# First loads of a retention kernel as two half-height transfers, issued from two engines

## The chip, the cores and the metric

The kernel runs on one core of a Trainium2 chip. The metric is device time in microseconds (us) of one execution, as a median of runs; lower is better. A core has TensorE (PE in the rows; its weight loads are PEld), VectorE (DVE), ScalarE (ACT), GpSimd (POOL), SyncE (SP, which here only issues transfers), and sixteen DMA engines that move data between device memory and the core.

## What is computed

The reference is a gated linear recurrence over 768 tokens (2 batches, 8 heads of 64), followed by two MLPs of 512 to 2048 to 512 on the resulting 1536 tokens:

```python
for t in range(S):
    state = gamma * state + einsum('bhd,bhe->bhde', k[:, :, t], v[:, :, t])
    y[:, :, t] = scale * einsum('bhd,bhde->bhe', q[:, :, t], state)
x = y.transpose(0, 2, 1, 3).reshape(1536, 512)
h = x @ w_in;  x = (h * tanh(softplus(h))) @ w_out
h = x @ w2_in; out = (h * cos(h)) @ w2_out
```

## The kernel before

The recurrence is done in twelve chunks of 128 tokens, six for each batch. A chunk's data are one row of the array `qkv`, 128 partitions by 2048 columns of float32 (1 MB): columns 0 to 1023 hold q and k transposed ("qk"), 1024 to 1535 hold v, 1536 to 2047 hold k in natural order ("k"). Here qk0 means qk of chunk 0, and so on; a qk load is 512 KB, a v or a k load of chunks 0 and 1 is 256 KB. From chunk 2 on v and k come as one load of 512 KB (vk2, vk3, ...). The constants ("few", 146 KB) come first; VectorE grows the causal mask from them, and GpSimd the decay factors.

For each chunk TensorE makes

- scores (`att_scores`, tile ps_s): needs qk; VectorE then multiplies the mask in (tile p);
- out (`att_out`, tile ps_y from p): needs p and v;
- update (`att_update`, tile ps_u): the running state, needs k and vd, which is v times a decay, made by GpSimd or, for chunks 1, 2, 4, 7 and 9, by ScalarE in eight instructions, one for each head;
- inter (`att_inter`, tile ps_y from qd and st): needs qd, made by GpSimd from q, and the state st of the chunk before.

After the twelve chunks (about 44 us) TensorE multiplies for the MLPs (tiles ps_h and ps_o) to the end. The MLP weights come through the same queue as the chunks; two weight loads stand among the chunk loads.

Every step is entered with `op(engine, cost, function, ...)` into a planner (`Plan`), which works out from the costs in what order the program is written; each engine then runs its instructions in that order. Loads are entered with engine "SP" and keep the order in which they are entered. All transfers of the kernel before are issued by SyncE and go through one hardware queue. Eight completion semaphores (DMAHW0 to DMAHW7 in the order below) are taken in turn, so a transfer can be issued only when the one eight places ahead of it has landed.

At the start there is nothing for TensorE to do: `start_up` gives it 24 multiplications of zeros (line 794), and the line `op("PE", 0.9, zeros, 8, "u")` puts 8 more between scores of chunk 0 and scores of chunk 1.

Of the kernel before, what the change touches and what calls it, by code (L numbers as in the profile page):

```python
# [10 lines left out]
F32 = mybir.dt.float32  # L11
F32R = mybir.dt.float32r
# [12 lines left out]
BLK = 512  # L25
# [46 lines left out]
class Plan:  # L72
# [15 lines left out]
    def op(self, engine, cost, fn, *args, needs=(), uses=(), new=None):  # L88
        n = len(self.ops)
        uses = list(uses)  # L90
        before = set(needs)
        reuse = None
        if new is not None:
            key, bufs, *tag = new
            line = self.lines.setdefault(tag[0] if tag else key[0], [])
            if line:
                before.add(self.owner[line[-1]])
            if len(line) >= bufs:
                reuse = line[-bufs]
            line.append(key)  # L100
            self.owner[key] = n
            uses.append(key)
        for key in uses:
            if self.owner.get(key, n) != n:
                before.add(self.owner[key])
            self.users.setdefault(key, set()).add(n)
        if engine in self.given:
            before |= {self.last[engine]} if engine in self.last else set()
            self.last[engine] = n
        att = fn.__name__.startswith("att") or fn.__name__ in ("start_up", "zeros", "load_consts")  # L110
        self.ops.append(dict(engine=engine, cost=cost, fn=fn, args=args, before=before, reuse=reuse, att=att))
        return n
# [64 lines left out]
def retention_two_mlps(ctx: ExitStack, tc: tile.TileContext, qkv, w1i, w1o, w2i, w2o, consts, out):  # L177
    nc = tc.nc
# [6 lines left out]
    g_p = ctx.enter_context(tc.tile_pool(name="g", bufs=3))  # L185
# [81 lines left out]
    att = {}  # L267
# [10 lines left out]
            x_t[m, j] = x_p.tile([128, 2, KD, BLK], F32R, tag="x", name="x")  # L278
        return x_t[m, j]

    def att_load(g, lo, hi, eng=nc.sync):
        if not att:
            t = x_p.tile([128, 2, KD, BLK], F32R, tag="x", name="qkv")
            for n in range(2):
                att[n] = t[:, n].rearrange("p a b -> p (a b)").bitcast(F32)
        elif g in IN_WO and g not in att:
            t = wo_p.tile([128, 2, 2, 512], F32R, tag="wo", name="qkv")
            att[g] = t.rearrange("p a b c -> p (a b c)").bitcast(F32)
        elif g in IN_G and g not in att:
            t = g_p.tile([128, 2, 2, BLK], F32R, tag="g", name="qkv")  # L290
            att[g] = t.rearrange("p a b c -> p (a b c)").bitcast(F32)
        elif g not in att:
            att[g] = att_p.tile([128, 2048], F32, tag="qkv", name="qkv", bufs=3)
        eng.dma_start(out=att[g][:, lo:hi], in_=qkv[g, :, lo:hi])  # L294

    def qk_of(g):
        return att[g][:, 0:1024].rearrange("p (a q b) -> p a q b", a=NPAIR, q=2)
# [237 lines left out]
    op = plan.op  # L535
# [48 lines left out]
    def chunk(g):  # L584
        return ("qkv", max(g, 1))

    def chunk_loads(g, cuts, queue=nc.sync):
        key = chunk(g)
        for lo, hi in zip(cuts, cuts[1:]):
            n = op(  # L590
                "SP", (hi - lo) * (0.00142 if g < 3 else 0.00122), att_load, g, lo, hi, queue,
                uses=[key], new=None if key in plan.owner else (key, 3, "x" if g < 2 else "wo" if g in IN_WO else "g" if g in IN_G else "qkv"),
            )
            for part, last in (("qk", 1024), ("v", 1536), ("k", 2048)):
                if lo < last and hi > last - 512:
                    at.setdefault((part, g), []).append(n)

    def chunk_pre(g):
        c = g % NCH
        key = chunk(g)  # L600
        on_act = g in VD_ACT
        if c + 1 < NCH:
            at["vd", g] = [
                op(
                    *(("ACT", 0.98) if on_act else ("POOL", 1.15)), att_vd, g, part, needs=at["v", g] + at["dec"],
                    new=None if part else (("vd", g), 2), uses=[key, ("vd", g)],
                )
                for part in range(2 if on_act else 1)
            ]
        if c > 0:  # L610
            name, cost, eng = ("DVE", 0.72, nc.vector) if g in QD_DVE else ("POOL", 1.95, nc.gpsimd)
            at["qd", g] = op(
                name, cost, att_qd, g, eng, needs=at["qk", g] + at["decq"], new=(("qd", g), 2), uses=[key]
            )
# [4 lines left out]
    def chunk_scores(g):  # L619
        s = [("s", g, e) for e in range(2)]  # L620
        if g == 1:
            s = [("s", g)] * 2
            at["s", g] = op("PE", 1.05, att_scores, g, needs=at["qk", g], new=(s[0], 1, "y"), uses=[chunk(g)])
        else:
            first = op(None, 0.0, nothing, new=(s[0], 3, "s"))
            at["s", g] = op("PE", 1.05, att_scores, g, needs=at["qk", g] + [first], new=(s[1], 3, "s"), uses=[chunk(g), s[0]])
        for e in range(2):
            at["p", g, e] = at["p", g] = op(
                "DVE", 0.71, att_mask, g, e, needs=[at["s", g]] + at["mask"],
                new=None if e else (("p", g), 2), uses=[s[e], ("p", g)],  # L630
            )
# [119 lines left out]
    few_t = []  # L751
# [7 lines left out]
        late_h_p = ctx.enter_context(tc.tile_pool(name="late_h", bufs=1, space=PSUM))  # L759
        o_p = ctx.enter_context(tc.tile_pool(name="o", bufs=2, space=PSUM))  # L760

    def load_consts():
        t = g_p.tile([128, 2, 2, BLK], F32R, tag="g", name="few").rearrange("p a b c -> p (a b c)").bitcast(F32)
        few_t.append(t)
        nc.sync.dma_start(out=t[:, 0:292], in_=consts[:, 0:292])  # L765

    def few(lo, n):
        return few_t[0][:, lo : lo + n]
# [22 lines left out]
    def zeros(n, tag):  # L791
        ps = ps_p.tile([128, 256], F32, tag=tag, name="ps_w")
        for _ in range(n):
            nc.tensor.matmul(ps, zero, zero[:, 0:1].to_broadcast([128, 256]), start=True, stop=True)

    def start_up():
        nc.vector.memset(zero, 0.0)
        nc.vector.memset(quarter, 0.25)
        nc.vector.memset(magic, MAGIC)
        nc.scalar.activation(out=spare, in_=quarter, func=AF.Copy, scale=quarter)  # L800
        zeros(2 * WARM, "u")

    at["close"] = op(None, 0.0, close)
    op("PE", 5.5, start_up)
    load = op("SP", 0.4, load_consts, new=("few", 3, "g"))
    chunk_loads(0, (0, 1024))
    for g in range(2):
        chunk_loads(g, (1024, 1536))
        chunk_loads(g + 1 + g, (0, 1024))
        chunk_loads(g, (1536, 2048))  # L810
        if g == 0:
            chunk_loads(2, (0, 1024))

    def later_loads(gs):
        for g in gs:
# [30 lines left out]
    for n in range(2):  # L846
        chunk_pre(n)
        chunk_scores(n)
        if n == 0:
            op("PE", 0.9, zeros, 8, "u")  # L850
    for n in range(NCHK):
        if 0 < n < NCHK - 1:
            chunk_pre(n + 1)
# [116 lines left out]
```

## Time and profile before

| | us |
|---|---|
| median of 3 runs | 571.52 (571.49 to 572.43) |
| the profiled execution's own time | 571.26 |
| span of the profiled execution, first to last instruction | 569.5 |
| TensorE busy in the span | 565.0 (99%) |
| VectorE, ScalarE, GpSimd busy | 384.4, 226.8, 97.7 |
| DMA queue q1, share of 16 engines' span | 23.6% |

The 1.8 us between the span and the profiled execution's time lie before the first and behind the last instruction of the program. The shares are averages over stages that differ much: in the first 42 us the DMA engines work without a break for most of the time, later they are mostly idle.

### The profile page before, as it was taken

The page shows a single profiled execution, that of the slowest core. Times are in us where ns is not written, and L with a number is a line of the kernel's source. Part 1 is how long each engine was busy: PE and PEld are TensorE (multiplying, and loading weights), DVE is VectorE, ACT ScalarE, POOL GpSimd, SP SyncE. Part 2 cuts the span into 40 slices and gives each one's busy share as a digit, 9 for nine tenths or more (in the row PEclk, how much of TensorE's full clock was granted, in tenths as well). Part 3 has the DMA queues.
Part 4 walks back from the last instruction along what each step waited for, and adds up shares of the span by engine and source line. Part 5 has one row for each costly group of instructions (what it writes and reads, how often), then busy time and mean ns, then how long its engine had stood idle before and what let it go on. Part 6 is the DMA issues. An engine that isn't in the chain of part 4 may idle for free.

```text
span 569.5 us, 7240 instructions
## 1 busy us (share of the span) xinstructions
PE 565.0 (99%) x3052; PEld 469.0 (82%) x3052; DVE 384.4 (67%) x420; ACT 226.8 (40%) x268; POOL 97.7 (17%) x74
## 2 busy tenths in 40 slices
PE   8999999999999999999999999999999999999997
PEld 6888888888888888888888888888888888888886
DVE  6689899652465527563487976898498894765462
ACT  2565443331312302304326466366246354354240
POOL 6770001111110201111101111122010311010000
PEclk9999999999999999999999999999999999999999
DMA  8982154421042200312022120303004100000203
GB/s 295 403 352 83 70 218 148 148 103 46 1 147 75 74 1 7 142 74 75 0 75 75 48 100 1 147 1 147 1 0 148 39 36 1 0 1 0 75 37 112
DMA packets 15008, 49.90 MB, mean 88 GB/s; under 512 B 1664, under 2 KB 2048, under 8 KB 14976
## 3 DMA queue, kind: packets, MB, share of 16 engines
q1 hardware_dynamic: 14976, 49.44, 23.6%
q8 instruction: 24, 0.39, 0.3%
q14 instruction: 8, 0.07, 0.0%
HBM read 46.29 MB, written 3.15 MB: 87 GB/s over the span
## 4 chain that ended last, share of the span: by engine, by line
PE 98%; DMA 1%; SPq 0%; DVE 0%; issue 0%
PE ps_h L431 46%; PE ps_o L454 46%; PE ps_y L384 2%; PE ps_s L329 2%; DMA qkv<-qkv_dram 1%; PE ps_y L374 1%; PE ps_u L345 1%; SPq L294 0%; DVE acc L520 0%; SPq L765 0%
## 5 line engine op out<-in xcount | busy, mean ns | idle before, releaser
L431 PE MATMUL ps_h<-x,wi 128*128 128x512 f32 x1152 | 264.8, 389 | 0.0
L431 PEld LDWEIGHTS ps_h<-x,wi 128*128 128x128 f32 x1152 | 216.2, 188 | 45.0 <-issue 0.2
L454 PE MATMUL ps_o<-wo,g 128*128 128x512 f32 (+1 forms) x588 | 132.5, 385 | 0.0
L454 PE MATMUL ps_o<-g,wo 128*128 128x512 f32 x576 | 132.4, 389 | 0.0
L454 PEld LDWEIGHTS ps_o<-wo,g 128*128 128x128 f32 x588 | 108.9, 188 | 22.0
L454 PEld LDWEIGHTS ps_o<-g,wo 128*128 128x128 f32 x576 | 108.1, 188 | 22.4
L262 POOL TENSOR_TENSOR wo<-mag,wo 128x1024 fp32r<-128x1024 f32 x14 | 35.8, 2559 | 211.4 <-ACT wo L248 158.4
L497 DVE TENSOR_TENSOR g<-mish,g 128x1024 fp32r<-128x1024 f32 x24 | 33.4, 1393 | 55.0 <-ACT g L493 55.0
L513 DVE TENSOR_TENSOR acc<-ps_o,acc 128x1024 f32<-128x1024 f32 x35 | 42.8, 1222 | 34.6 <-PE ps_o L454 34.4
L262 POOL TENSOR_TENSOR wi<-mag,wi 128x1024 fp32r<-128x1024 f32 x12 | 30.3, 2526 | 193.1 <-ACT wi L248 193.1
L464 ACT ACTIVATE mish<-ps_h 128x1024 f32<-128x1024 f32 (+1 forms) x25 | 24.9, 995 | 95.7 <-PE ps_h L431 95.7
L477 DVE SCALAR_TENSOR_TENSOR turns<-whole,turns 128x1024 f32<-128x1024 f32 x24 | 29.3, 1223 | 44.7 <-ACT whole L473 44.7
L469 ACT ACTIVATE turns<-ps_h,quarter 128x1024 f32<-128x1024 f32 x24 | 26.7, 1113 | 65.4 <-PE ps_h L431 65.1
L239 DVE SCALAR_TENSOR_TENSOR mag<-raw,mag 128x1024 uint32<-128x1024 uint32 (+1 forms) x38 | 42.2, 1111 | 1.2
L486 ACT ACTIVATE turns<-turns 128x1024 f32<-128x1024 f32 x24 | 25.5, 1062 | 34.8 <-DVE turns L483 34.6
L497 DVE TENSOR_TENSOR g<-turns,g 128x1024 fp32r<-128x1024 f32 x24 | 33.2, 1383 | 8.0 <-ACT g L493 8.0
L489 DVE TENSOR_TENSOR turns<-turns,ps_h 128x1024 f32<-128x1024 f32 x24 | 29.2, 1216 | 10.1 <-ACT turns L486 6.8
L254 DVE SCALAR_TENSOR_TENSOR mag<-raw,mag 128x1024 uint32<-128x1024 uint32 x26 | 33.8, 1301 | 0.4
L493 ACT CAST g<-turns 128x1024 fp32r<-128x1024 f32 x24 | 25.1, 1045 | 17.0 <-DVE turns L489 16.8
L248 ACT CAST wi<-mag 128x1024 fp32r<-128x1024 f32 (+1 forms) x20 | 17.4, 872 | 26.5 <-DVE mag L254 22.4
L473 ACT ACTIVATE whole<-turns,magic 128x1024 f32<-128x1024 f32 x24 | 27.7, 1153 | 0.8
L483 DVE TENSOR_SCALAR turns<-turns 128x1024 f32<-128x1024 f32 x24 | 27.0, 1126 | 0.8
(50 smaller groups left out, 326.6 us busy)
## 6 DMA issues: line engine op xcount, KB each, us to landing
qkv<-qkv_dram SPq DMA_DIRECT2D x22, 512.0 KB, 10.0
raw<-w1i_dram SPq DMA_DIRECT2D x16, 512.0 KB, 4.2
raw<-w1o_dram SPq DMA_DIRECT2D x16, 512.0 KB, 4.1
raw<-w2i_dram SPq DMA_DIRECT2D x16, 512.0 KB, 3.7
raw<-w2o_dram SPq DMA_DIRECT2D x16, 512.0 KB, 3.7
out_dram<-acc SPq DMA_DIRECT2D x11, 256.0 KB, 2.1
qkv<-qkv_dram SPq DMA_DIRECT2D x4, 256.0 KB, 7.1
out_dram<-acc SPq DMA_DIRECT2D x2, 128.0 KB, 1.7
```

The lines of the kernel that those rows point to most:

```text
L239: nc.vector.scalar_tensor_tensor(out=a, in0=high, scalar=0xC0000000, in1=a, op0=ALU.bitwise_and, op1=ALU.bitwise_or)
L254: nc.vector.scalar_tensor_tensor(out=w_all_of(it, single)[:, ns], in0=raw_t[it][:, ns, :, 0], scalar=29, in1=mag_t[it][:, ns], op0=ALU.log ...
L262: eng.tensor_sub(out=w[:, :, 1], in0=w_all_of(it, single)[:, ns].bitcast(F32), in1=w[:, :, 0].bitcast(F32))
L431: nc.tensor.matmul(h[:, 0 if h_tag(k) == "s" else f % 2, :], w[:, f % 2, a, kk * 128 : (kk + 1) * 128], x[:, b, kk, :], start=(a + b + kk ...
L454: nc.tensor.matmul(ps, lhs, rhs, start=(n == 0), stop=(n == 3 * GF - 1))
L469: nc.scalar.activation(out=t_t[k], in_=h_t[k], func=AF.Identity, scale=INV_2PI, bias=quarter)
L473: nc.scalar.activation(out=n_t[k], in_=t_t[k], func=AF.Identity, bias=magic)
L477: nc.vector.scalar_tensor_tensor(out=t, in0=n_t[k], scalar=MAGIC, in1=t, op0=ALU.subtract, op1=ALU.subtract)
L483: nc.vector.tensor_scalar(out=t, in0=t, scalar1=-0.5, scalar2=0.5, op0=ALU.max, op1=ALU.min)
L489: nc.vector.tensor_mul(out=t_t[k], in0=t_t[k], in1=h_t[k])
L497: nc.vector.tensor_sub(out=g[:, :, 1, :], in0=t_t[k], in1=g[:, :, 0, :].bitcast(F32))
L513: nc.vector.tensor_add(out=acc, in0=o_t[m * NG + G, j, p], in1=acc)
```

## The change

The constants and qk0, qk1 and qk2 are each loaded by two transfers, partitions 0 to 63 by SyncE and partitions 64 to 127 by ScalarE. k0 stays one transfer and is issued by ScalarE. The order becomes few, qk0, qk1, then v0 (SyncE) and k0 (ScalarE), qk2, v1, qk3, k1; before it was few, qk0, v0, qk1, k0, qk2, v1, qk3, k1. ScalarE issues its five transfers at the head of `start_up`. The 8 multiplications of zeros ahead of scores of chunk 1 become 4. The planner's cost of an early load goes from 0.00142 to 0.0013 us a column.

```diff
+    early = []
+    issued = set()
+    EVERY, UPPER, LOWER = slice(0, 128), slice(0, 64), slice(64, 128)
+
-    def att_load(g, lo, hi, eng=nc.sync):
+    def att_load(g, lo, hi, eng=nc.sync, at_rows=EVERY):
...
-        eng.dma_start(out=att[g][:, lo:hi], in_=qkv[g, :, lo:hi])
+        if (g, lo, hi, at_rows) not in issued:
+            eng.dma_start(out=att[g][at_rows, lo:hi], in_=qkv[g, at_rows, lo:hi])
+            issued.add((g, lo, hi, at_rows))
...
-    def chunk_loads(g, cuts, queue=nc.sync):
+    def chunk_loads(g, cuts, queue=nc.sync, at_rows=EVERY):
...
-                "SP", (hi - lo) * (0.00142 if g < 3 else 0.00122), att_load, g, lo, hi, queue,
+                "SP", (hi - lo) * (0.0013 if g < 3 else 0.00122) * share, att_load, g, lo, hi, queue, at_rows,
...
+            if queue is not nc.sync:
+                early.append((g, lo, hi, queue, at_rows))
...
-    def load_consts():
+    def load_consts(eng=nc.sync, at_rows=UPPER):
...
-        nc.sync.dma_start(out=t[:, 0:292], in_=consts[:, 0:292])
+        eng.dma_start(out=few_t[0][at_rows, 0:292], in_=consts[at_rows, 0:292])
...
     def start_up():
+        load_consts(nc.scalar, LOWER)
+        for load in early:
+            att_load(*load)
...
-    chunk_loads(0, (0, 1024))
     for g in range(2):
-        chunk_loads(g, (1024, 1536))
-        chunk_loads(g + 1 + g, (0, 1024))
-        chunk_loads(g, (1536, 2048))
-        if g == 0:
-            chunk_loads(2, (0, 1024))
+        chunk_loads(g, (0, 1024), at_rows=UPPER)
+        chunk_loads(g, (0, 1024), nc.scalar, LOWER)
+    chunk_loads(0, (1024, 1536))
+    chunk_loads(0, (1536, 2048), nc.scalar)
+    chunk_loads(2, (0, 1024), at_rows=UPPER)
+    chunk_loads(2, (0, 1024), nc.scalar, LOWER)
+    chunk_loads(1, (1024, 1536))
+    chunk_loads(3, (0, 1024))
+    chunk_loads(1, (1536, 2048))
...
-            op("PE", 0.9, zeros, 8, "u")
+            op("PE", 0.45, zeros, 4, "u")
```

The change moves instructions at three places. On SyncE, at the head of the program, the loads of the kernel before stand in this order (few, qk0, v0, qk1, k0, qk2, v1, qk3, k1, vk2):

```order
L765 DMA few<-consts_dram 128x292
L294 DMA qkv<-qkv_dram 128x1024
L294 DMA qkv<-qkv_dram 128x512
...
L294 DMA qkv<-qkv_dram 128x512 [waits DMAHW0_49]
L294 DMA qkv<-qkv_dram 128x1024 [waits DMAHW1_49]
```

In the changed kernel SyncE issues the upper halves of few, qk0 and qk1, v0, the upper half of qk2, then v1, qk3, k1 and vk2:

```order
L775 DMA few<-consts_dram 64x292
L299 DMA qkv<-qkv_dram 64x1024 x2
L299 DMA qkv<-qkv_dram 128x512
L299 DMA qkv<-qkv_dram 64x1024 [waits DMAHW1_49]
L299 DMA qkv<-qkv_dram 128x512 [waits DMAHW2_49]
L299 DMA qkv<-qkv_dram 128x1024 [waits DMAHW3_49]
L299 DMA qkv<-qkv_dram 128x512 [waits DMAHW4_49]
L299 DMA qkv<-qkv_dram 128x1024 [waits DMAHW5_49]
```

The eight semaphores are now taken by halves, so the first wait comes earlier in the list: the upper half of qk2 waits for the upper half of the constants, v1 and qk3 for the two halves of qk0, k1 and vk2 for those of qk1.

On ScalarE, at the head of the program, the kernel before has

```order
L965 UNCONDITIONAL_BRANCH [waits barrier_Pool_Activation_PE_DVE_SP_release]
L800 ACT_TABLE_LOAD
L800 ACTIVATE spare<-quarter 128x1 [waits DVE_49]
L398 CAST x<-ps_y 128x2x2x128 [waits PE_49]
L308 ACTIVATE vd<-qkv,cst 128x64 [waits DMAHW6_49,Pool_49]
```

and the changed kernel the lower halves of few, qk0 and qk1, then k0, the lower half of qk2, and only then the table load:

```order
L775 DMA few<-consts_dram 64x292
L299 DMA qkv<-qkv_dram 64x1024 x2
L299 DMA qkv<-qkv_dram 128x512
L299 DMA qkv<-qkv_dram 64x1024 [waits DMAHW0_49]
L813 ACT_TABLE_LOAD
L813 ACTIVATE spare<-quarter 128x1 [waits DVE_49]
L404 CAST x<-ps_y 128x2x2x128 [waits PE_49]
```

The table load and the one activation behind it moved back past five transfers, the last of which waits for the lower half of the constants.

On TensorE, from the last multiplications of zeros to update of chunk 0, the kernel before has eight such pairs of a weight load and a multiplication (the last one stands here) and then

```order
L794 LDWEIGHTS zero
L794 MATMUL ps_w<-zero 128x256
L329 MATMUL ps_s<-qkv 128x128 [waits DMAHW3_49]
L329 MATMUL ps_s<-qkv 128x128 x7
L384 MATMUL ps_y<-p,qkv 64x128 [waits DMAHW2_49,DVE_49]
L384 MATMUL ps_y<-p,qkv 64x128 [waits DVE_49]
L384 MATMUL ps_y<-p,qkv 64x128 x6
L345 MATMUL ps_u<-vd,qkv 64x64 [waits DMAHW4_49,PE_49,Pool_49]
```

and the changed kernel four such pairs and then

```order
L804 LDWEIGHTS zero
L804 MATMUL ps_w<-zero 128x256
L335 MATMUL ps_s<-qkv 128x128 [waits DMAHW5_49]
L335 MATMUL ps_s<-qkv 128x128 [waits DMAHW4_49]
L335 MATMUL ps_s<-qkv 128x128 x6
L390 MATMUL ps_y<-p,qkv 64x128 [waits DMAHW7_49,DVE_49]
L390 MATMUL ps_y<-p,qkv 64x128 [waits DVE_49]
L390 MATMUL ps_y<-p,qkv 64x128 x6
L351 MATMUL ps_u<-vd,qkv 64x64 [waits DMAHW6_49,PE_49,Pool_49]
```

Scores of chunk 1 now wait for both halves of qk1 (DMAHW5 and 4), out of chunk 0 for v0 (DMAHW7), update of chunk 0 for k0 (DMAHW6) and for vd of GpSimd. Nothing else moves: the instructions of VectorE, GpSimd and TensorE stand in the same order as before to the end of the program.

## Rows read from the trace of the kernel before

**Rows 1.** The page: span, and busy time of each engine with share and count

```profile
span 569.5 us, 7240 instructions
PE 565.0 (99%) x3052; PEld 469.0 (82%) x3052; DVE 384.4 (67%) x420; ACT 226.8 (40%) x268; POOL 97.7 (17%) x74
```

**Rows 2.** The chain that ended last, in order of time: start us, us, what

```profile
2.10 6.57 DMA qkv<-qkv_dram
...
9.87 1.02 PE ps_y L384 x16
...
13.48 0.60 PE ps_y L374 x16
...
31.63 0.47 PE ps_u L345 x16
...
544.55 21.92 PE ps_o L454 x108
566.50 0.42 DVE acc L520
```

**Rows 3.** The timeline of TensorE, 0 to 12 us

```profile
0.99 5.15 PE L794 MATMUL ps_w<-zero 128*128 128x256 bf16 x24 [0.99 <-DVE magic L799]
6.07 1.16 PE L329 MATMUL ps_s<-qkv 64*128 64x128 f32 x16
7.16 1.06 PE L794 MATMUL ps_w<-zero 128*128 128x256 bf16 x8
8.71 1.16 PE L329 MATMUL ps_s<-qkv 64*128 64x128 f32 x16 [0.49 <-DMA qkv<-qkv_dram]
```

**Rows 4.** ScalarE's vd of chunk 7, TensorE's update of chunk 7

```profile
29.47 2.02 ACT L308 ACTIVATE vd<-qkv,cst 128x64 f32<-128x64 f32 x8 [1.44 <-DMA qkv<-qkv_dram]
31.46 0.63 PE L345 MATMUL ps_u<-vd,qkv 128*64 128x64 f32 x16
```

**Rows 5.** Busy time by stretch: DMA share and GB/s stand last

```profile
1.00:2.00 1.00, 1.00 (x5) 0.70 (x6) 0.00 (x0) 1.00 (x1) 0.00 (x0) 1.00 0.15 27
2.00:3.00 1.00, 1.00 (x7) 0.71 (x5) 0.00 (x0) 0.31 (x2) 0.00 (x0) 1.00 0.86 266
3.50:5.50 2.00, 2.00 (x12) 1.38 (x10) 1.83 (x6) 0.00 (x0) 1.60 (x6) 1.00 0.84 191
8.00:12.00 4.00, 3.51 (x62) 3.10 (x62) 2.35 (x5) 1.06 (x4) 3.38 (x5) 1.00 1.03 402
16.00:30.00 14.00, 14.00 (x278) 12.21 (x275) 10.35 (x19) 5.99 (x19) 10.74 (x15) 1.00 1.02 406
```

**Rows 6.** Line 294, one issue each: v0 at 1.6 us, k0 at 2.6

```profile
L294 SPq DMA_DIRECT2D qkv<-qkv_dram x1: 424/424/424, 1.6 to 1.6; - x1
...
DMA to landing us min/median/max: 5.2/5.2/5.2
...
L294 SPq DMA_DIRECT2D qkv<-qkv_dram x1: 432/432/432, 2.6 to 2.6; - x1
...
DMA to landing us min/median/max: 6.7/6.7/6.7
```

**Rows 7.** The timeline of GpSimd: vd of chunk 0, qd of chunk 1

```profile
7.44 1.04 POOL L305 TENSOR_TENSOR vd<-qkv,cst 128x512 f32<-128x512 f32 x1
8.81 0.73 POOL L313 TENSOR_TENSOR qd<-qkv,cst 128x256 f32<-128x256 f32 x1 [0.33 <-DMA qkv<-qkv_dram]
9.62 1.52 POOL L316 TENSOR_TENSOR qd<-qkv,cst 64x256 f32<-64x256 f32 x2
```

**Rows 8.** The timeline of VectorE and of ScalarE at the start

```profile
7.26 1.29 DVE L336 TENSOR_TENSOR p<-ps_s,cst 128x512 f32<-128x512 f32 x2 [0.26 <-PE ps_s L329]
...
0.73 1.28 ACT L800 ACT_TABLE_LOAD   x1 [0.73 <-PEq L959]
...
10.94 0.58 ACT L398 CAST x<-ps_y 128x512 fp32r<-128x512 f32 x1 [8.63 <-PE ps_y L384]
```

**Rows 9.** SyncE's first two issues: constants in the timeline, qk0 by line

```profile
0.74 0.37 SPq L765 DMA_DIRECT2D few<-consts_dram  x1
...
L294 SPq DMA_DIRECT2D qkv<-qkv_dram x1: 421/421/421, 1.2 to 1.2; - x1
```

More of the change, by code (lines that the diff above doesn't have):

```diff
@@ L585, in chunk @@
         return ("qkv", max(g, 1))
-    def chunk_loads(g, cuts, queue=nc.sync):
+    def chunk_loads(g, cuts, queue=nc.sync, at_rows=EVERY):
         key = chunk(g)
+        share = (at_rows.stop - at_rows.start) / 128
         for lo, hi in zip(cuts, cuts[1:]):
             n = op(
-                "SP", (hi - lo) * (0.00142 if g < 3 else 0.00122), att_load, g, lo, hi, queue,
+                "SP", (hi - lo) * (0.0013 if g < 3 else 0.00122) * share, att_load, g, lo, hi, queue, at_rows,
                 uses=[key], new=None if key in plan.owner else (key, 3, "x" if g < 2 else "wo" if g in IN_WO else "g" if g in IN_G else "qkv"),
             )
+            if queue is not nc.sync:
+                early.append((g, lo, hi, queue, at_rows))
             for part, last in (("qk", 1024), ("v", 1536), ("k", 2048)):
@@ L760, in close @@
         o_p = ctx.enter_context(tc.tile_pool(name="o", bufs=2, space=PSUM))
-    def load_consts():
-        t = g_p.tile([128, 2, 2, BLK], F32R, tag="g", name="few").rearrange("p a b c -> p (a b c)").bitcast(F32)
-        few_t.append(t)
-        nc.sync.dma_start(out=t[:, 0:292], in_=consts[:, 0:292])
+    def load_consts(eng=nc.sync, at_rows=UPPER):
+        if not few_t:
+            t = g_p.tile([128, 2, 2, BLK], F32R, tag="g", name="few")
+            few_t.append(t.rearrange("p a b c -> p (a b c)").bitcast(F32))
+        eng.dma_start(out=few_t[0][at_rows, 0:292], in_=consts[at_rows, 0:292])
     def few(lo, n):
```

## The prediction, made before the changed kernel ran

> **What bounds the kernel now.** I read the page first, then the chain of waits, then the timeline of the first 45 us engine by engine. The page says that TensorE is busy 565.0 of 569.5 us [rows 1]. The chain says where the rest is: it waits for qk1, which is issued at 2.10 and takes 6.57 us to land, and from scores of chunk 1 at 8.71 it stays on TensorE, piece behind piece, to 566.50, where one addition of VectorE and the last store follow [rows 2, 3]. So the time is: the moment at which scores of chunk 1 start, plus a fixed 557.8 us of multiplications, as long as no later piece has to wait. A change of the loads can only move that start, or put a new wait behind it. Ahead of it TensorE runs 24 zero products (0.99 to 6.14), scores of chunk 0 at 6.07, eight zero products at 7.16 to 8.22, and idles 0.49 us for qk1 [rows 3].
>
> The second thing to see is that the transfers run nearly in step with TensorE. From 8 us on the sixteen DMA engines are full, at 402 to 406 GB/s; before that they are much slower, 27 GB/s in the second microsecond, 266 in the third, 191 from 3.5 to 5.5 [rows 5]. A consumer late in this stretch shows how little room there is: ScalarE's vd of chunk 7 idled 1.44 us for its load and started when it landed, at 29.47; its eight heads are done at 31.49, and TensorE's update of chunk 7, which reads them one by one, starts at 31.46 [rows 4]. The update takes 0.47 us of the chain [rows 2], so the eighth head is read at about 31.46 + 7/8 x 0.47 = 31.87. With 0.04 us from a landing to a start (8.67 to 8.71 [rows 2, 3]) the room is 31.87 - 31.49 - 0.04 = 0.34 us. That load's landing is set by the bytes ahead of it in a full stream, and the change does not alter their number.
>
> **The change, part by part.**
>
> *Order of need.* Ahead of qk1's landing stand few, qk0 and qk1: 146 + 512 + 512 = 1170 KB instead of 1426 with v0. v0 (the first 914 KB) landed at 1.6 + 5.2 = 6.8, qk1 (1426 KB) at 8.67 [rows 2, 6]; at that pace 1170 KB are there at 6.8 + 256/512 x 1.87 = 7.74.
>
> *Four zero products fewer.* Eight take 1.06 us [rows 3], so four save 0.53, and scores of chunk 1 can start at 8.22 - 0.53 = 7.69 at the earliest. That is the ceiling of the whole change: 8.71 - 7.69 = 1.02 us, 0.18% of the time. It is cover work that nothing reads, and what it hid was the wait for qk1.
>
> *v0 moves back.* It now comes behind qk1, and beside k0 on the other queue. If the two queues get equal shares, v0 lands with k0, when 1682 KB are through; k0 landed there at 2.6 + 6.7 = 9.3 before [rows 6]. Out of chunk 0 needs it, and started at 9.87 [rows 2]. If scores start at 7.74 and take 1.16, TensorE is ready for out at 8.9 and waits to 9.34: of the 0.97 gained, 0.53 stay. The masked scores p are no hindrance (done 8.55 [rows 8]).
>
> *GpSimd behind v0.* vd of chunk 0 takes 1.04 us, then qd of chunk 1 takes until 2.33 us after its start (8.81 to 11.14) [rows 7]. With v0 at 9.3 that is 10.38 and 12.71. Update of chunk 0 would follow out, at 9.34 + 1.02 = 10.36, which fits; inter of chunk 1 stood at 13.48 [rows 2] and would stand at 12.95, which leaves 0.24. GpSimd is late next if v0 is later still.
>
> *ScalarE.* Five issues stand ahead of the table load. SyncE's issue of 128 partitions took 0.37 to 0.42 us [rows 9], so 2.1 us at most, plus the wait for its half of the constants; the table load of 1.28 then ends before 5. ScalarE's first real work is at 10.94 [rows 8], so 6 us of idle time hide this. If that were gone, it would cost the 2.1 us.
>
> *SyncE's earlier waits.* v1 and qk3 now wait for qk0's halves (about 6 us), k1 and vk2 for qk1's (about 7.7). v0, k0 and qk2, 1 MB or 2.6 us at 402 GB/s, are queued by then, so the DMA engines do not run dry: nothing.
>
> *Two issuers.* No row shows a transfer of 64 partitions or a second queue. Against a loss stands nothing in the rows, so the bounds are wide. For a gain: from 1 to 3 us the DMA engines are not full (0.15 and 0.86 [rows 5]); qk0's issue ends 0.42 us after the constants' because one engine issues both [rows 9]. Halves issued side by side could bring the stream forward by 0 to 0.42 us; I take 0.2, half of the one issue. The slow stretch from 3.5 to 5.5 is not explained by issue (k0 had been issued at 2.6 [rows 6]); if two queues cured it, 0.38 MB would take 0.94 instead of 2 us, a gain of 1.06. If they made a half-height transfer run at half of 406 GB/s, the stream would be late by 1.2 us or more (below).
>
> **The sum.** Three limits apply, and the smallest gain counts: scores of chunk 1 (0.97, by the 1.02 ceiling with the stream 0.2 earlier), v0 (9.87 - 9.34 = 0.53, and 0.73 with 0.2), and vd of chunk 7 (0.34, and 0.54 with 0.2). What scores gain at the start is lost again in front of v0 and of chunk 7's update, since everything on TensorE is queued behind that update. The gain is 0.54 us: 571.26 - 0.54 = 570.72 for a run like the profiled one, which lay 0.26 under the median; from the median 571.52 it is 570.98, and I predict 571.0.
>
> [...]
>
> **Rivals.**
>
> *1. Half-height transfers run at half rate.* The slow side. The pairs hold 146 + 3 x 512 = 1682 KB = 1.72 MB; at 203 GB/s, half of the full stream, they take 8.5 us from 2.0 on, and v0 and k0 (0.52 MB) 1.3 us more: qk2 lands at 11.8. Before it was there at k0's 9.3 plus 512 KB at 406 GB/s, 10.6. All later loads are 1.2 us late, the room of 0.34 is used up, and the time rises by 0.86 to 572.4; if the slow start adds its 1.06 on top, 573.4. I take 572.8. It decides from 1.48 us of delay (0.34 + 1.14) to be slower by more than 0.2%. For it: the early stream is slow for a reason not seen. Against: the two halves together cover all 128 partitions, and both queues are filled at the same time. 13%.
>
> *2. The slow start is cured.* The stream is 0.7 to 1 us early, neither v0 nor chunk 7 waits, and the gain is the ceiling of 1.0: 570.5. For it: 191 GB/s with full queues is far from 402. Against: nothing says that more queues help full DMA engines. 22%.
>
> *3. The stream does not move, or moves back by up to half a microsecond,* because the other half comes later or is slower. Then update of chunk 7 takes nearly all: +0.34 to -0.2, about 571.4. That is the change not doing what it does at the start. 20%.
>
> *The forecast* holds the remaining 45%, with a range of its own of 570.7 to 571.3.
>
> **Numbers.** About 0.2% (1.14 us) is what a measurement of this kernel can tell from no change. Faster needs more than the ceiling, or rival 2 with a favourable median: a third of its 22%, and little else: 0.08. Slower is more than half of rival 1 and a tail of rival 3: 0.09. Same is 0.83. The range from 570.3 to 572.5 holds the forecast, rivals 2 and 3, and the lower part of rival 1.
>
> **What would show it.** In the profile after: scores of chunk 1 at 7.5 to 7.8 with less than 0.2 us of idle time; out of chunk 0 waiting for v0 up to about 9.1; a wait of 0.2 to 0.5 us at update of chunk 7 for ScalarE's vd; ScalarE's table load at 2.5 to 4.5 with nobody waiting. The DMA rate from 2 to 8 us tells rivals 1 and 2 from the forecast. The prediction is wrong if that rate falls or rises by more than a sixth, or if an idle stretch of TensorE ahead of 10 us lets its granted clock fall from 1.00, which the 0.49 us idle before scores of chunk 1 did not do [rows 3, 5].

## The result, and the profile after

The changed kernel took 574.88 us (median of six runs, 573.90 to 577.23) against 571.61 us for the kernel before in the same session: ratio 1.006, 95% interval 1.0038 to 1.0081. It is 3.3 us slower, and the prediction of 571.0 us (570.3 to 572.5) was wrong in sign and size. The profiled execution took 574.73 us with a span of 572.9, against 571.26 and 569.5 [rows 1].

The chain that ended last in the changed kernel, in order of time (start us, us, what), set against [rows 2]:

```profile
2.89 9.85 DMA qkv<-qkv_dram
12.74 0.14 issue
12.87 0.69 PE ps_u L351 x16
...
15.99 0.60 PE ps_y L380 x16
...
34.28 0.99 PE ps_u L351 x16
...
547.73 21.92 PE ps_o L460 x108
...
569.68 0.42 DVE acc L526
```

The chain no longer begins with qk1 but with k0, which ScalarE issued at 2.89 and which took 9.85 us to land. Set the same pieces side by side. Update of chunk 0 stood behind out of chunk 0 at 9.87 + 1.02 = 10.89 [rows 2] and now starts at 12.87: 1.98 us late. Inter of chunk 1 stood at 13.48 and stands at 15.99: 2.51 late. Update of chunk 7 stood at 31.63 and stands at 34.28, 2.65 late, and takes 0.99 instead of 0.47: what follows is 3.17 late. From there nothing is added: the last long piece starts at 547.73 instead of 544.55, 3.18 late. So nearly the whole loss is made in the first 35 us (the two profiled executions differ by 3.47 us; the other 0.29 lie behind the last addition or outside the program's instructions). At update of chunk 7 the eight heads come from ScalarE, which waits for its load:

```profile
32.87 2.02 ACT L314 ACTIVATE vd<-qkv,cst 128x64 f32<-128x64 f32 x8 [2.14 <-DMA qkv<-qkv_dram]
```

It started at 29.47 before [rows 4], so this load is 3.40 us late. Less the room of 0.34 that the prediction worked out, that is 3.06 us; the chain shows 3.17. The consumer was right, the delay of the stream was not. Some 0.7 of the 3.40 us belong to that load alone: it landed 2.0 us after the load ahead of it (at 32.8 and 30.8), where 1.25 us lay between the same two before (29.4 and 28.1). Such slow transfers stand in other profiled executions too, at different places (before: 2.2 us, landing at 16.5; the new order with whole transfers: 2.1 and 2.3 us). Without this one the 2.65 us from the start would have been the delay, an estimate. TensorE's timeline at the start, against [rows 3]:

```profile
6.22 1.93 PE L335 MATMUL ps_s<-qkv 64*128 64x128 f32 x16
8.07 0.62 PE L804 MATMUL ps_w<-zero 128*128 128x256 bf16 x4
8.74 0.49 PE L335 MATMUL ps_s<-qkv 64*128 64x128 f32 x2
9.68 1.16 PE L335 MATMUL ps_s<-qkv 64*128 64x128 f32 x14 [0.46 <-DMA qkv<-qkv_dram]
10.78 1.09 PE L390 MATMUL ps_y<-p,qkv 128*64 128x128 f32 x16
12.87 0.69 PE L351 MATMUL ps_u<-vd,qkv 128*64 128x64 f32 x16 [1.00 <-DMA qkv<-qkv_dram]
```

Two things are new. Scores of a chunk that came in halves break in two: the first two products start on the first half, and the other fourteen wait for the second (8.74 and 9.68). And update of chunk 0 waits 1.00 us for k0. Why all this is late is seen in the busy time by stretch (DMA share and GB/s stand last), against [rows 5]:

```profile
3.50:5.50 2.00, 2.00 (x12) 1.38 (x10) 1.76 (x8) 0.97 (x1) 1.61 (x7) 1.00 0.88 135
8.00:12.00 4.00, 3.36 (x38) 2.43 (x36) 2.38 (x4) 0.09 (x1) 1.29 (x2) 1.00 1.05 262
1.00:16.00 15.00, 13.39 (x128) 9.98 (x132) 8.48 (x17) 4.06 (x11) 8.76 (x16) 1.00 0.94 251
16.00:30.00 14.00, 14.00 (x282) 12.11 (x284) 9.32 (x17) 6.81 (x22) 10.67 (x15) 1.00 1.02 406
```

The DMA engines are as busy as before (1.05 from 8 to 12 us, 1.03 before), but move 262 GB/s instead of 402. From 16 us on, with the last half landed, they are back at 406. The row from 1 to 16 us gives one number that serves for all runs below. In the kernel before it was:

```profile
1.00:16.00 15.00, 14.51 (x184) 11.53 (x186) 9.39 (x19) 5.67 (x18) 10.83 (x19) 1.00 0.94 323
```

(323 - 251) x 15 us = 1.08 MB had not yet arrived at 16 us, and at 406 GB/s these take 2.7 us. I call this the lag of the stream.

Two smaller things. Issuing became dearer, not cheaper: SyncE's first issues of 128 partitions took 0.37 and 0.42 us [rows 9], and the first four of line 299 take 0.47 to 0.59 on SyncE and 0.60 to 0.96 on ScalarE (columns are min/median/max in ns, then the first and last start):

```profile
L299 ACTq DMA_DIRECT2D qkv<-qkv_dram x4: 602/747/962, 1.3 to 3.5; - x4
L299 SPq DMA_DIRECT2D qkv<-qkv_dram x4: 465/580/589, 1.4 to 3.2; - x4
```

Not all of this is the number of partitions: v0 and k0, with 128, are among them at 0.59 and 0.60. The loads alone (below) show the number by itself: the first issue of a stage took SyncE 0.33 to 0.39 us with 128 partitions and 0.47 to 0.54 with 64.

And TensorE's mean granted clock was 1.0 in three of the six runs (573.90, 574.50, 574.73 us) and 0.997 in the other three (575.03, 576.33, 577.23). In the profiled run it was 1.00 throughout, so the clock is no part of the account above.

### The profile page after: what moved, and what is told of

It is laid out like the page before. It is cut to its first block, busy times and chain, and to the rows that moved or that the text cites. A ratio compares the mean times of both kernels' runs of the same rounds, so it can differ in the third digit from the quotient of the medians.

```text
span 572.9 us, 7239 instructions
## 1 busy us (share of the span) xinstructions
PE 567.0 (99%) x3048; PEld 470.1 (82%) x3048; DVE 384.6 (67%) x420; ACT 227.0 (40%) x268; POOL 97.6 (17%) x74
## 4 chain that ended last, share of the span: by engine, by line
PE 97%; DMA 2%; ACTq 0%; DVE 0%; issue 0%
PE ps_h L437 46%; PE ps_o L460 46%; PE ps_s L335 2%; PE ps_y L390 2%; DMA qkv<-qkv_dram 2%; PE ps_y L380 1%; PE ps_u L351 1%; ACTq L299 0%; ACTq L775 0%; DVE acc L526 0%
## 5 line engine op out<-in xcount | busy, mean ns | idle before, releaser
L483 DVE SCALAR_TENSOR_TENSOR turns<-whole,turns 128x1024 f32<-128x1024 f32 x24 | 29.4, 1223 | 44.7 <-ACT whole L479 44.7
```

What stands on the lines that cost most here:

```text
L483: nc.vector.scalar_tensor_tensor(out=t, in0=n_t[k], scalar=MAGIC, in1=t, op0=ALU.subtract, op1=ALU.subtract)
```

## The experiments

Theory A: 64 neighbouring partitions (0 to 63, or 64 to 127; no others were tried) are slow to load by themselves, whatever the queue. Rival B: the second queue, or the interleaving of two transfers, is slow. Theory C concerns the gain that did not come: the new order helps at the start, but something later gives it back.

### What about the pairs is slow: queue, size or which partitions

All three keep the order of the changed kernel. One issues the halves all by SyncE:

```diff
-        chunk_loads(g, (0, 1024), nc.scalar, LOWER)
+        chunk_loads(g, (0, 1024), nc.sync, LOWER)
...
-    chunk_loads(0, (1536, 2048), nc.scalar)
+    chunk_loads(0, (1536, 2048))
```

> The changed kernel with all transfers issued by SyncE, through one queue; halves and order as in the change. Theory A (a transfer of 64 partitions is itself slow, the second queue does no harm): the stream stays at 200 to 300 GB/s until qk2 has landed, after 12.5 us, and the time is 574 us or more. Theory B (two queues on the same DMA engines hinder each other): the stream is back at the pace of the kernel before, qk2 lands before 11 us, and the time is 571.0 to 571.6.

One keeps both queues and cuts the pairs by columns, so that each transfer has 128 partitions and half of the bytes of a row:

```diff
-        chunk_loads(g, (0, 1024), at_rows=UPPER)
-        chunk_loads(g, (0, 1024), nc.scalar, LOWER)
+        chunk_loads(g, (0, 512))
+        chunk_loads(g, (512, 1024), nc.scalar)
...
```

(and in the same way the constants and qk2)

> The changed kernel with the pairs cut by columns: both halves have 128 partitions, with 512 columns each (146 for the constants), one half by SyncE and one by ScalarE, in the same order. Theory A: the pairs run at full pace, qk2 lands at 10.3 to 10.8 us, 571.0 to 571.5. Theory B: 200 to 300 GB/s until qk2 has landed, after 13 us, 574 to 575.

One keeps both queues and 64 partitions per transfer, but takes the even and the odd ones, which are no neighbours. If the neighbourhood is what counts, they have full pace; if any 64 partitions are slow, that of the changed kernel:

```diff
-    EVERY, UPPER, LOWER = slice(0, 128), slice(0, 64), slice(64, 128)
+    EVERY, UPPER, LOWER = slice(0, 128), slice(0, 128, 2), slice(1, 128, 2)
...
```

> The changed kernel with the pairs cut into even and odd partitions: still 64 partitions a transfer and two queues, but each half reaches over all 128 partitions. [...] Theory A in the form that any transfer of 64 rows is slow: as the changed kernel, 574 to 575. Theory B: 574 to 575 too.

Busy time by stretch, 8 to 12 us and 1 to 16 us, of the halves issued by one queue:

```profile
8.00:12.00 4.00, 4.00 (x38) 3.12 (x37) 1.63 (x3) 0.00 (x0) 1.94 (x3) 0.63 1.05 238
1.00:16.00 15.00, 12.85 (x122) 10.11 (x124) 8.12 (x17) 3.20 (x9) 8.57 (x16) 0.89 0.90 231
```

Of the column halves in two queues:

```profile
8.00:12.00 4.00, 3.73 (x64) 3.32 (x64) 2.74 (x6) 1.05 (x3) 2.48 (x4) 1.00 1.05 405
1.00:16.00 15.00, 14.68 (x184) 11.47 (x186) 9.59 (x20) 6.05 (x18) 9.95 (x17) 1.00 0.94 320
```

Of the even and odd partitions in two queues:

```profile
8.00:12.00 4.00, 3.54 (x58) 3.00 (x58) 2.77 (x5) 0.59 (x1) 2.46 (x3) 1.00 1.03 398
1.00:16.00 15.00, 14.03 (x174) 10.94 (x176) 9.25 (x18) 5.36 (x15) 9.96 (x17) 1.00 0.90 308
```

One queue does not cure it: 575.94 us, ratio 1.0077 (1.0058 to 1.0095), 238 GB/s (three of its four runs have a mean granted clock of 0.997; the fourth took 575.05). Two queues with column halves have the full rate (405) and 572.33 us, 1.0012 (1.0003 to 1.0021). Two queues with 64 partitions each, but every second one, have 398 GB/s and 572.69 us, 1.0019 (1.0009 to 1.003). So neither the second queue nor the number of partitions of a transfer is the cause of the 3 us: B falls, and it is the neighbourhood that lowers the rate. A rest of 0.44 and 0.80 us, whose intervals leave out zero, stays with these two kernels and is not explained.

### The loads alone

This kernel leaves the whole computation out. It loads 8 x 512 KB of the same input in each of ten stages, and the next stage waits for the one before:

```python
def halves_two_queues(g):
    load(g, nc.sync, UPPER)
    load(g, nc.scalar, LOWER)
...
for n, stage in enumerate(stages):
    for g in range(8):
        stage(g)
    nc.vector.tensor_copy(out=mark[:, n], in_=big[:, :, 0])
```

> The whole computation is left out: ten stages of eight loads of 512 KB each and nothing beside them, each stage started when the stage before has landed (stage 5 loads only partitions 0 to 63, so 256 KB each). Theory A (64 neighbouring partitions of SBUF are slow by themselves, whatever queue and whatever the rest of the kernel does): whole transfers in one or two queues, even and odd partitions in two queues, and column halves in two queues run at 380 to 420 GB/s, as the stream after 8 us did; neighbouring halves run at 200 to 270 in two queues and in one; the upper half alone at about 200. Rival B (it was the start of the kernel, other transfers or TensorE's reads that made them slow): all stages at about 400, neighbouring halves too. Rival C (two queues filled at once even the halves out, and only the order in time hurts): halves in two queues at 350 to 420, in one queue at 200 to 270, upper alone about 200. The first stage also shows whether the slow start (191 GB/s from 3.5 to 5.5 us) is there without any computation: then stage 1 is slower than stage 2, which is the same.

Busy time by stretch within the stages (the kernel uses only VectorE and GpSimd beside the DMA engines; GB/s last). In this order: whole transfers at the start of the kernel and later in that stage, whole transfers at the start of the second stage and later in it, halves in two queues, halves in one queue, the upper half alone, even and odd in two queues, whole ones in two queues, halves in two queues again:

```profile
3.50:5.50 2.00, 0.00 (x0) 0.00 (x0) 1.00 0.86 207
8.00:12.00 4.00, 0.00 (x0) 0.00 (x0) 1.00 1.02 417
18.50:20.50 2.00, 0.00 (x0) 0.00 (x0) 1.00 0.91 248
23.00:28.00 5.00, 0.00 (x0) 0.00 (x0) 1.00 1.02 414
34.00:44.00 10.00, 0.00 (x0) 0.00 (x0) 1.00 1.00 274
55.00:65.00 10.00, 0.00 (x0) 0.00 (x0) 1.00 1.04 239
73.00:80.00 7.00, 0.00 (x0) 0.00 (x0) 1.00 1.02 210
87.00:93.00 6.00, 0.00 (x0) 0.00 (x0) 1.00 1.01 385
115.00:122.00 7.00, 0.00 (x0) 0.00 (x0) 1.00 0.99 394
131.00:141.00 10.00, 0.00 (x0) 0.00 (x0) 1.00 1.04 265
```

Without any computation, and long after the start, the halves have the rates that they had in the kernel: 265 to 274 GB/s in two queues (262 there), 239 in one (238 there), 210 for one half alone. Even and odd halves and whole transfers have 385 to 417. Theory A holds, and both rivals named for this run (its C: two queues even the halves out) fall. The column stage can't be read: ScalarE had issued its loads during the stage before. The rows answer a second question too. The slow start of the kernel before (191 GB/s from 3.5 to 5.5 us [rows 5]) is there without the computation (207), and again when the second stage starts on idle DMA engines (248 from 18.5 to 20.5, then 414). So in both stages it came in the first microseconds after the engines had stood idle, and not at the start of the kernel alone; what makes it is not shown. It is not always there: in the profiled runs of two kernels below, in which ScalarE issues a single transfer, at the same moment as SyncE its first, the stream had 301 and 284 GB/s from 3.5 to 5.5 us.

### How much of it is needed

First the changed kernel with qk2 alone in halves (512 KB of 1682; the constants and chunks 0 and 1 whole, by SyncE, so that qk2's lower half is ScalarE's only issue and goes out at the start; its tile is then allocated by that load), then the changed kernel with qk2 alone whole (1170 KB in halves):

```diff
-        chunk_loads(g, (0, 1024), at_rows=UPPER)
-        chunk_loads(g, (0, 1024), nc.scalar, LOWER)
+        chunk_loads(g, (0, 1024))
...
-    chunk_loads(0, (1536, 2048), nc.scalar)
+    chunk_loads(0, (1536, 2048))
...
```

> The new order, whole transfers but for queries and keys of chunk 2, which are cut at partition 64 and issued by SyncE and ScalarE (512 KB in halves instead of 1682). Theory A (each byte in neighbouring halves costs the stream the same extra time: 3.2 us for 1682 KB in the changed kernel, so 0.97 us for 512 KB): chunk 2's queries and keys land about 11.5 instead of 10.6, all loads behind by about 1 us, time 0.3 to 1.0 us above the kernel before, 572.2 to 572.9. Rival D (the loss comes from the slow first microseconds, where the constants and chunk 0 are in halves): no loss, 571.9 as with the new order alone.

```diff
-    chunk_loads(2, (0, 1024), at_rows=UPPER)
-    chunk_loads(2, (0, 1024), nc.scalar, LOWER)
+    chunk_loads(2, (0, 1024))
```

> The changed kernel with queries and keys of chunk 2 in one transfer of 128 partitions; constants and chunks 0 and 1 still in halves (1170 KB of 1682). Theory A: 3.2 x 1170/1682 = 2.2 us late at chunk 2's queries and keys, so they land at about 12.8 and the time is 2.0 to 2.4 us above the kernel before, 573.8 to 574.3. Rival D (the loss comes from the slow first microseconds): the full 3 us remain, 574.9. If the falling granted clock of some runs of the changed kernel comes from TensorE's wait for chunk 1, it is here too.

Busy time by stretch with qk2 alone in halves:

```profile
5.50:8.00 2.50, 2.12 (x24) 1.46 (x22) 2.36 (x3) 0.00 (x0) 2.29 (x3) 1.00 0.91 312
10.00:12.00 2.00, 1.40 (x30) 1.04 (x25) 0.96 (x3) 0.59 (x1) 1.92 (x3) 1.00 1.02 225
1.00:16.00 15.00, 13.38 (x158) 10.32 (x158) 8.93 (x18) 4.98 (x13) 9.84 (x17) 1.00 0.96 296
```

And with qk2 alone whole:

```profile
3.50:5.50 2.00, 2.00 (x12) 1.42 (x10) 1.14 (x6) 1.58 (x2) 1.01 (x5) 1.00 0.95 191
5.50:8.00 2.50, 2.50 (x24) 1.81 (x22) 2.40 (x4) 0.00 (x0) 2.22 (x4) 1.00 0.99 243
10.00:12.00 2.00, 2.00 (x42) 1.88 (x40) 1.15 (x2) 0.12 (x1) 1.75 (x3) 1.00 1.02 407
1.00:16.00 15.00, 13.97 (x156) 10.90 (x156) 8.85 (x18) 5.10 (x14) 9.23 (x16) 1.00 0.94 297
```

The slow stretch goes where the halves are: at 10 to 12 us with qk2 halved, at 5.5 to 8 with chunks 0 and 1 halved, and the other stretch has 312 and 407 GB/s. The first has the size that theory A expected: lag (323 - 296) x 15 / 406 = 1.0 us, and 572.76 against 571.86 us, 1.0011 (1.0002 to 1.0021). It is no clean pair, though: the lower half landed at 4.44, the upper one at 12.13, so the slow stretch is that of an upper half beside whole transfers. The second missed: 572.92 us, 1.0018 (1.0008 to 1.0027), 1.06 us slower instead of 2.0 to 2.4, lag 0.96. A rate of "so much for each byte in halves" is too simple. From 3.5 to 5.5 us this kernel had 191 GB/s, as much as the kernel before, where whole transfers were slow too; in that stretch of this execution the halves cost nothing. Rival D (all of the loss comes from the first microseconds) falls with both.

The lags at 16 us, 1.0 and 0.96, don't add up to the 2.7 of the changed kernel. Cut at 8 us they nearly do. Busy time from 1 to 8 us, of the kernel before, the changed one, qk2 alone in halves and qk2 alone whole:

```profile
1.00:8.00 7.00, 7.00 (x48) 5.02 (x48) 4.43 (x11) 1.31 (x2) 4.38 (x10) 1.00 0.82 238
1.00:8.00 7.00, 6.90 (x40) 4.79 (x40) 3.71 (x10) 1.58 (x2) 3.85 (x9) 1.00 0.82 180
1.00:8.00 7.00, 6.62 (x44) 4.65 (x44) 4.11 (x10) 1.58 (x2) 3.86 (x9) 1.00 0.86 263
1.00:8.00 7.00, 7.00 (x44) 5.00 (x44) 3.54 (x9) 1.58 (x2) 3.23 (x9) 1.00 0.83 190
```

At 8 us the changed kernel is (238 - 180) x 7 / 406 = 1.0 us behind and loses 1.7 more up to 16. With qk2 alone whole it is 0.8 and 0.1. With qk2 alone in halves the stream is 0.4 us ahead at 8 us and then loses 1.4. So the halves of the constants, qk0 and qk1 cost 0.8 to 1.0 us and those of qk2 1.4 to 1.7, and that the lag of the kernel with qk2 in halves met the 0.97 of theory A was luck. All this is one execution each, and such lags scatter: the second row of the table is a kernel without any halves. The times, medians of several runs, are the safer evidence.

| kernel | KB in neighbouring halves | lag at 16 us, us | time against before, us | the same, runs with a granted clock of 0.999 or 1.0 alone, us |
|---|---|---|---|---|
| new order, whole transfers | 0 | 0.3 | +0.04 | +0.04 (11 of 11) |
| the same, ScalarE's work on the first weight load held | 0 | 0.8 | +0.08 | +0.08 (11 of 11) |
| column halves, two queues | 0 | 0.1 | +0.44 | +0.44 (10 of 10) |
| even and odd, two queues | 0 | 0.6 | +0.80 | +0.73 (9 of 10) |
| qk2 in halves | 512 | 1.0 | +0.90 | +0.90 (10 of 10) |
| constants, qk0, qk1 in halves | 1170 | 1.0 | +1.06 | +0.98 (9 of 10) |
| the changed kernel | 1682 | 2.7 | +3.27 | +2.89 (3 of 6) |
| its halves in one queue | 1682 | 3.4 | +4.05 | +3.16 (1 of 4) |

### The new order without halves

```diff
-        chunk_loads(g, (0, 1024), at_rows=UPPER)
-        chunk_loads(g, (0, 1024), nc.scalar, LOWER)
+        chunk_loads(g, (0, 1024))
```

(and in the same way the constants, k0 and qk2, all issued by SyncE; the four zero products fewer stay)

> The changed kernel with whole transfers of 128 partitions, all by SyncE; what stays is the new order (qk1 ahead of v0 and k0) and four zero products instead of eight. Both theories: the stream keeps the pace of before, scores of chunk 1 start at about 7.75 us, out of chunk 0 waits for v0 until about 8.9, update of chunk 7 for ScalarE's vd. Gain 0.34 us by the room before that update, 571.2 against 571.6. If the room was read wrongly, the gain is 0.8 to 1.0.

571.93 us, ratio 1.0002 (0.9993 to 1.001): no gain. Scores of chunk 1 do start earlier, at 7.95 instead of 8.71. But the timelines of ScalarE, VectorE and TensorE show a wait behind it that the prediction did not look for:

```profile
27.56 0.69 ACT L216 ACTIVATE mag<-raw 128x512 f32<-128x512 f32 x1 [2.98 <-DMA raw<-w1i_dram]
28.15 0.58 ACT L404 CAST x<-ps_y 128x512 fp32r<-128x512 f32 x1
...
28.76 0.69 DVE L407 TENSOR_TENSOR x<-ps_y,x 128x512 fp32r<-128x512 f32 x1 [2.26 <-ACT x L404]
29.36 1.28 DVE L342 TENSOR_TENSOR p<-ps_s,cst 128x512 f32<-128x512 f32 x2
...
30.10 1.16 PE L335 MATMUL ps_s<-qkv 64*128 64x128 f32 x14 [0.39 <-DVE p L342]
```

ScalarE is held by the first weight load (2.98 us); the cast behind it, VectorE's addition and p queue up, and scores of chunk 8 wait 0.39 us. The first p starts 0.74 us ahead of these scores; in the kernel before p started at 28.68, and the same 0.74 ends at 29.42, while its scores of chunk 8 started at 29.52. That is a room of 0.10 us, or some 0.24 with the two products ahead of the third, which is the one that waits (an estimate, 2/16 of the 1.09 us of these scores): tighter than the 0.34 at update of chunk 7. Here ScalarE had the load at 27.56 against 26.88 before; two transfers ahead of it landed 2.1 and 2.3 us after the one before them, where 1.25 is usual (in the kernel before one did, with 2.2). Three kernels test whether this is what gives the gain back: ScalarE's work on the first weight load held until one cast later, that load itself moved behind chunk 7's loads, and the same move in the kernel before. The first two start from the new order with whole transfers.

```diff
-    hold(at["act", i00, 0], at["xh", 4])
+    hold(at["act", i00, 0], at["xh", 5])
```

> The order-only kernel (e2) with one more edit: ScalarE's absolute value of the first weight load stands behind its cast of chunk 5 instead of ahead of it. Theory C (in e2 ScalarE, which works in order, waits for that load and so holds back the cast, VectorE's products for chunk 7 and scores of chunk 8): the wait at scores of chunk 8 is gone, what is left is the wait of update of chunk 7 for vd, and the time is 0.2 to 0.4 us below e2, 571.5. Theory D (the gain of e2 is lost by other means, such as a stall of the loads that comes by chance): no change against e2, the wait stays in place.

```diff
-    later_loads((4, 5, 6))
-    weight(("i", 0, 0), lambda: later_loads((7, 8, 9)))
+    later_loads((4, 5, 6, 7))
+    weight(("i", 0, 0), lambda: later_loads((8, 9)))
...
-    hold(at["act", i00, 0], at["xh", 4])
+    hold(at["act", i00, 0], at["xh", 6])
+    hold(at["vd", 9][0], at["act", i00, 0])
```

> The order-only kernel (e2) with the first weight load (512 KB) issued behind the loads of chunk 7 instead of ahead of qk8 and vk7, and its absolute value behind ScalarE's cast of chunk 5. Theory C: both waits behind the start are relieved by 1.26 us of transfer, and the gain at the start (scores of chunk 1 at 7.7 to 8.0 instead of 8.71) reaches the end: 0.6 to 0.9 us below the kernel before, about 571.1. Theory D: as e2, 571.9.

> The kernel before with the same move of the first weight load and nothing else. Theory C: scores of chunk 1 start at 8.71 as before and nothing behind them waits in either kernel, so the time is that of before within 0.2 us. Theory D gives no reason for a gain either; a gain here would say that the load's place alone had cost time.

Times: 571.94 (1.0001, 0.9992 to 1.0009), 571.93 (1.0001, 0.9992 to 1.001), and 571.77 for the kernel before with the move (0.9998, 0.9989 to 1.0007). In the traces the wait at scores of chunk 8 is gone in both; with the load moved, TensorE waits for nothing after scores of chunk 1 (its waits in total, times, longest):

```profile
PE ps_w L804 <- DVE magic L811: 1.0, 1, 1.0
PE ps_s L335 <- DMA qkv<-qkv_dram: 0.2, 1, 0.2
```

That profiled run took 570.96 us, 0.30 less than the one of before, but it is the fastest of its eleven (to 572.58), and their median is 0.07 us above that of before. So the wait is real, and taking it away is worth nothing that these runs resolve. Theory C, which expected 571.5 and 571.1, is not borne out by the times; why the earlier start does not reach the median is not shown.

The last one of this group adds to the new order with the load moved that ScalarE issues the constants (one transfer of 128 partitions), so that qk0 is SyncE's first issue:

```diff
+        load_consts(nc.scalar)
...
-    load = op("SP", 0.4, load_consts, new=("few", 3, "g"))
+    load = op("SP", 0.4, nothing, new=("few", 3, "g"))
```

> e6 with the constants issued by ScalarE, whole, beside SyncE's first load qk0. Theory C: SyncE's issues start 0.42 us earlier, the stream is 0 to 0.4 us earlier, and the time is 0 to 0.3 us below e6. If two queues with whole transfers hindered each other, it would be slower than e6.

It is slower: 573.78 us, 1.0024 (1.0014 to 1.0033). But its eleven runs fall into two groups: five with a granted clock of 1.0 took 572.19 to 573.01 us (median 572.33, 0.47 above the kernel before), and six with 0.996 or 0.997 took 573.78 to 574.04. So the late constants by themselves cost about 0.5 us, and the rest of the 1.9 comes with the lower clock. The chain of the profiled run, one of the first group, begins

```profile
0.74 4.63 DMA few<-consts_dram
```

and goes on through the mask on VectorE to out of chunk 0, which waits for p:

```profile
10.21 0.43 PE L390 MATMUL ps_y<-p,qkv 128*64 128x128 f32 x2 [1.30 <-DVE p L342]
```

The constants landed at 5.37 instead of some 3.0; qk0, issued at the same moment on the other queue, landed at 5.20. Here the transfer that was needed first came 2.4 us later with a large one beside it on the other queue.

### The granted clock

The changed kernel with more zero products in its two waits (12 instead of 4 ahead of scores of chunk 1, 7 ahead of update of chunk 0):

```diff
-            op("PE", 0.45, zeros, 4, "u")
+            op("PE", 0.45, zeros, 12, "u")
...
+        if n == 0:
+            op("PE", 0.1, zeros, 7, "u")
```

> The changed kernel, loads as in it, with 12 instead of 4 zero products ahead of scores of chunk 1 and 7 more ahead of update of chunk 0, which fill TensorE's 0.46 and 1.00 us of waiting for the late stream. If the runs of the changed kernel with a mean granted clock of 0.997 come from that waiting, all runs have 0.999 or 1.0 here and the median is that of its undisturbed runs, about 574.5 (2.5 to 2.9 above the kernel before): the rest of the loss is the late stream alone. If the clock falls for another reason, a part of the runs has 0.997 again and the median stays at 574.9 or more.

All five runs have a mean granted clock of 0.999 or 1.0 and lie within 574.65 to 575.38; the median is 574.96, ratio 1.0053 (1.0039 to 1.0067). Its waits are not gone: in the profiled run, whose stream is later still, update of chunk 0 waits 0.21 us instead of 1.00, but scores of chunk 1 wait 0.52 instead of 0.46, and scores of chunks 0 and 2 wait 0.33 and 0.24. Five of five against three of six speaks for the waits as what let the clock fall, and for the fall as what made the runs of 576 and 577 us, without proving either. The median does not gain: the late stream alone is worth 3.1 us here, with a lag of 3.4 us at 16 us in the profiled run. The one profiled run in which it falls early is that of the halves in one queue. There TensorE had been idle 1.26 us up to 7.27, and then its granted clock was 0.51 and 0.50, instead of 1.00 up to there, for some 3 us (in the last two rows the third number from the right):

```profile
7.27 1.87 PE L335 MATMUL ps_s<-qkv 64*128 64x128 f32 x14 [1.26 <-DMA qkv<-qkv_dram]
7.50:9.00 1.50, 1.50 (x14) 1.35 (x12) 0.53 (x2) 0.00 (x0) 0.77 (x1) 0.51 0.98 197
9.00:10.90 1.90, 1.90 (x13) 1.29 (x14) 1.06 (x2) 0.00 (x0) 0.57 (x1) 0.50 1.14 282
```

Such an idle stretch does not always do it: with the constants issued by ScalarE TensorE idled the 1.30 us shown above, and the clock stayed at 1.00 in that run, while it fell in six of the eleven. With qk2 alone whole, where TensorE waits 0.8 us for chunk 1, one run of ten shows a fall (0.996).

## Why the prediction was wrong

The step that failed is **two issuers** with its rival 1: the sum took the stream to be 0.2 us earlier, and half-height transfers to be no slower as a pair, because "the two halves together cover all 128 partitions, and both queues are filled at the same time". They are slower: the stream was 2.7 us late at 16 us, and the loads alone show why: 265 to 274 GB/s for the pair, 239 in one queue, 210 for one half, 385 and more as soon as each transfer holds partitions from both halves. Which partitions a half holds is what counts: even and odd halves have 398 GB/s in the kernel and 385 in the loads alone, both halves in flight. Two neighbouring halves together ran at 1.14 times (239, one queue) and 1.30 times (274, two) the 210 of one alone. What makes neighbouring halves slow is not shown. In every run the rows of the source are cut together with the partitions, so these runs do not tell whether the neighbourhood counts where the data are written or where they are read.

**Rival 1** had the slow pairs, at 13%, but priced them too low, 572.8 (573.4 with the slow start on top; 574.88 came). Its 203 GB/s, an estimate that no row of before shows, was not the error: pairs ran a little faster (239 to 274 in the loads alone). Three things were missing. The slow start came on top of the halves: from 1 to 8 us the stream had 180 GB/s against 238 before. v0 and k0, whole transfers beside the pairs, were priced at 402 GB/s and shared the 262 of the stretch. And the lateness of qk2 was taken from the bytes ahead of it alone, while later loads (v1 and qk3, issued at 7.0 and 7.3) are in flight at the same time. The two halves of qk2 landed at 13.0 and 13.8 instead of 11.8, and the lag was 2.7 us at 16 us, and 3.4 at chunk 7's load, instead of 1.2.

**From lag to time** was right: the room of 0.34 at update of chunk 7 and the rule that the rest of TensorE's work just follows (3.40 - 0.34 = 3.06, measured 3.17, though 2.65 of it was there before that update). What it missed is the tighter place at scores of chunk 8, by way of ScalarE's wait for the first weight load; it took the order's gain in one trace, and the kernels without it are no faster.

**Order of need**: qk1 alone was taken to land at 7.74; with whole transfers scores of chunk 1 started at 7.95, 8.25 and 8.36 in three profiled runs. In the changed kernel the second half landed just ahead of 9.68.

**Four zero products fewer** was called cover that nothing reads. With whole transfers in one queue it cost nothing: all 33 runs of three such kernels have a granted clock of 0.999 or 1.0. With late halves TensorE waits 0.46 and 1.00 us, and the clock falls in half of the runs (0.997 in three of six); in the last experiment, whose 15 zero products more leave 0.52 us as the longest wait, it stays up (0.999 or 1.0 in all five). The four that the change leaves out could have covered the first wait only; what they are worth by themselves is not shown. The prediction named an idle stretch as what would make it wrong, and did not price it.

**ScalarE's issues** took longer than 0.42 us each (0.57 to 0.96), and its table load started at 4.53 and ended at 5.81 instead of before 5, but nobody waited for it. **GpSimd behind v0** was late, as it was said it would be if v0 were late: vd of chunk 0 idled 2.81 us and started at 10.71 instead of 7.44 [rows 7]. In the chain it is hidden behind k0, which landed 2 us later still. **SyncE's earlier waits** cost nothing that a run shows. The column halves have them too (v1 issued at 6.2 us, in the changed kernel at 7.0, with whole transfers in the new order at 3.8), and there the DMA engines are full (1.05 from 8 to 12 us) and the lag is 0.1 us. Whether a part of that kernel's 0.44 us comes from them is not shown.

## What to carry to other kernels

Before splitting a transfer between queues, ask which partitions each piece holds: if it must be split, cut by columns, or by even and odd rows, not into partitions 0 to 63 and 64 to 127 (here 405 and 398 GB/s against 262 from 8 to 12 us; and no split was faster than whole transfers, 572.33 us at best against 571.93). A full share of busy DMA engines does not mean a full rate (1.05 with 262 GB/s, 1.03 with 402); read share and GB/s side by side, stretch by stretch. Where a stream of loads feeds a full TensorE, the cost of a slow load was here about its lag less the tightest room of any consumer behind it (3.40 - 0.34 = 3.06 us, measured 3.17), and rooms must be searched on every engine that waits for a load, not only at the consumer that idles most.

## What had not been expected of the hardware

- The slow first microseconds of loading came back after the DMA engines had been idle: 207 GB/s in the first stage of the loads alone, 248 in the second, against 414 to 417 later in each. In two kernels they were not there (301 and 284 GB/s); what makes them is open.
- An issue of 64 partitions took longer than one of 128: as the first of a stage of the loads alone 0.47 to 0.54 us on SyncE against 0.33 to 0.39.
- A small transfer on one queue came late beside a large one on another: the constants landed at 5.37 instead of 3.0 us when qk0 came in beside them (one profiled run).
